# One set of 64x64 score products per tile, keys and queries of the two head halves on row halves of shared tiles

## The chip, the core and the metric

The kernel runs on one core of a Trainium2 chip. The metric is device time in microseconds (us). PE is TensorE, DVE VectorE, ACT ScalarE, POOL GpSimd, SP SyncE, whose queue issues the DMA transfers.

## The reference

Four batches of eight heads, 768 positions, head width 64. Each position attends to a window of 15 positions on either side and to 24 block summaries (the block's largest key, its mean value); a layer norm and a two-layer network with a residual follow.

```python
B, H, S, D = q.shape                      # 4, 8, 768, 64
block, window = (32, 16)
k_sum = k.reshape(B, H, nb, block, D).max(axis=3)
v_sum = v.reshape(B, H, nb, block, D).mean(axis=3)
scores_l = scale * np.matmul(q, k.transpose(0, 1, 3, 2))
mask_l = np.abs(pos[:, None] - pos[None, :]) < window
scores_s = scale * np.einsum('bhsd,bhnd->bhsn', q, k_sum) + np.log(block)
# softmax over both kinds of scores, then a @ concatenate([v, v_sum])
x = np.ascontiguousarray(attn_out.transpose(0, 2, 1, 3)).reshape(B, S, H * D)
xn = (x - mu) / np.sqrt(var + 1e-06) * g_ln
ch = np.maximum(xn @ w_ch1, 0.0) @ w_ch2
return x + ch
```

## The kernel before

**Tiles and stages.** A tile T is 128 positions with all eight heads; there are 24, six a batch. Batch 0 (T = 0 to 5) runs in f32 (steps early_k, early_qk, softmax, early_transp, early_pv), while the weights are fetched, merged and split into f16 high and low parts. Batches 1 to 3 (T = 6 to 23) run with high and low f16 parts. T has two head halves, hh = 0 and 1, of four heads (j) each; t = 2T + hh.

**A late tile.** load_q(t) (line 419) brings the queries of one half into the staging tile qs, twice, once into each 64 of the 128 partitions, with two transfers of 128 KB. ACT casts them to f16 in all 128 partitions, DVE overwrites the first 64 with the low part. load_k(t) (432) brings the keys of the window, already doubled over the two partition halves, in one transfer of 368 KB into ksg; ACT makes kh, DVE the low part kl. heads(T, hh) (455) multiplies over 128 rows, so that a product with kh adds low and high queries at once: for each j, one product with kh and one with kl for either half of the 64 output columns, which begin at key columns that fit that half of the positions. These are 16 products of 128 rows by 64 columns, with 120 moving columns, into one PSUM bank, s0 for hh = 0 and o0 for hh = 1. late_softmax(t) (503) masks and takes the minimum on DVE, exponentiates on ACT, splits into high and low on ACT and POOL, and turns the result by a transposing DMA. values(T) (469), called two tiles later (LAG), has 48 products of 128 rows by 64 columns over 64 moving columns (o). late_out(T) (610) normalises, ln(T) (622) and lnT(T) (638) make the layer norm and turn it by a transposing DMA into xt, of which one covers two tiles, a group g.

**The network.** g1(s) (758), with s = 8g + j, makes 256 hidden columns for a group in two halves of 12 products of 128x128 over 256 columns (h). g2 and, from group 3, g2_wide (827) multiply by the second weights; a g2_wide step has 21 products of 256 columns (acc_a, acc_s, acc_o).

**Batch steps.** batch_k, batch_q, batch_v (294 to 368) load a batch ahead of its tiles and find block summaries and scales; batch_kput (405) casts the key summaries into the border columns of kh and kl of one head half; four POOL copies for each second pair of heads double the summaries over the partition halves (318).

**The order.** The steps don't issue at once. Plan.record notes each operation, a unit() of products counting as one, and issue() (158) emits them in the order of a packed table, ORDER (58): each number in it is the place of an operation in the noted list. The engines' queues run in that order. All instructions carry line 163 for this reason.

**Buffers.** work() (173) gives a tag and a number of buffers to the pool. qs and ksg have one buffer; the f16 queries one for each hh; late["k", hh] is one pair kh, kl for each hh.

Of the kernel before, what the change touches and what calls it, by code (L numbers as in the profile page):

```python
# [13 lines left out]
F32 = mybir.dt.float32  # L14
# [10 lines left out]
P = 128  # L25
# [5 lines left out]
NC = 184  # L31
# [27 lines left out]
    "c-lRf2Y8O>+s3c^36Vr%#9p-`{EZ4RG7v>+O3~J))cg=lt+raNRn=;#)i$<P`Pb~Qil`A1TVj<8DMjqjBqWi%_x1gr*LQqJjyLamp8LMWd7jsKze"  # L59
    "Z}wHEk&8^}G}6aip5$YZ394LiK1-$>Mc!UYF(5yXq^Y<)Zpas9fih05RUbbxvQ8k+QtnrL)XtTT1q-k*1QWRU}F_>k`Mva8FzLM@vZ^xvRaMuRJx"  # L60
    "Sr?c3Tt$%anEHl~GAcj<DtS3pQnlm<CL*)fIrvdUrUzAha_f!kCDW3$%0Uc>l>^*HO_w<gIVbus;mFICz>q<S7VJ~ZSvM6r;vX3=dikgcyR5Ep#^"
    "R}nAJmijtT0*k9I*QeQ*H^?xRR7U>Cevo9kF*w#RO5LLHEGB?H?*3hv3_}(r{iUqPBMk|cTI2(c^a7%-D)SwA@<9at@bB*M_Zd_T3e>;44I~}a#u"
    "R*32iPX)R7XzP{m}~a5=8u>vwWVbM!ZDBc)i~-&E8qdQ-beh8WG4CpJOX$r<h7Z1!|^vTUlgQjc0iI|-g9@<3aA>%NBCoYT?HLmQ=wWVEj2eFS@*"
    "kwJP=Rom)N36uJ!DADiH`X<WzX%nfgE2M<^)23;E<E!_zq*-g<Hbx8R=rY@d-Zn9ZwUt^8aFXe40~2V1ZEgKlqMUzi5jm!@W}AJ<_}d)0V;f4gN%"
    "q7_5qWG%+UxWuM$eG@Sv^PhFR<Q5X~~{HN?*-3mpzxIpB~p6;NvJr>dGr41@<^73lnRDoG5!;&+2jM$Z7^u9FthHMWa=1O$lVJIeJPf%T28yxAX<"
    "sp^k~Aa!X9K475i<XnEPqXZ69}0proiR`sT&Xm16%rh!f4wMrj*-_)@_lE&VLb-w;A`!!Eq))WvIDNXf|9047X`i1$%ZZ#g8&3!{ORgan&^)r$7b"
    "IFpP^3<m22ijN$%QKy%du5FF2R)(sgS@R*B!owv8WU&Z$hC`Bloe77)})w1eaR-tYq|@hwIau4Q`=rLF?KF{Z(`jcwvSnFmzW}&ua9kIr>U(cYh<"
    "?+(FR)4MC)O?*&dF?N*Hy@w6#nnDW{pbLGDONzDd!?GQ;jSskSGTIxbapsp$$gO6UP|&`yEZjvSVK`m$8itLBh>AU)K|UfUV|z9JEtA;shi=>r0c"
    "{4KY=+}aAZXUexkdrRg>I|<gBa#lPVYcFUu6Qn8df3b8HAFV=dOKAhSDV6mD(_K4&gGJJd=Rc@+dC=Qj|3Y8x>OE>zS9h3lME<@$;xAI;%?^8jJ4"
    "5BNey3N=7W=yS$~rJ9TocS|wwkLGFeF53Xrcs~r+n8=ugXy=uP=kxG)b4f_JC<)Z}aMVU1EJ@r3sNJ8)d#j!8)t^?nf=uaa>y;^vA-NMKVEapn%`"  # L70
    "Vdb^WO7&##g<e0S7v(mz@HgDU(W|T(gVH07k4mIECHO=L_k@f<SrE4Cn3ev{vveHNPn07YFr0Q6kBCXlw0R1l{yYgB~E=i0{hHDOZKPY2tCXDw1C"
    "6V@!Nh7LWT7^7E+r#MJH7TY^GTt7NHag!#2-ipy>xFBQxxsFMlF7O^)KxztwdJ5j!lzH90!q_ba&29+ABEgUG|gnTnd&Jm+o*r2l-65%U22NxQE3"
    "LA3w5rHwKdFr_AlW1iGANp)>4`ylcW<_e`=<}_F0-}X4y$H-Ig)|Qdc_3Y-&)Pj?J)BovEIe%?TZ67TdaV#wtv`Y1^AWbvSx(TF27w$+nX@r^Czw"
    "6vfZ{k2zusG}XTAEaZKF$+ZR2Ou}WA4L28cjdl@Veb+qFVEI-H?FQL_8t&Jo+R^dVFWF})eIIW8b&mBnKj@co(z>-TVtUCsJJ!sz&8XKC{lPXiS9"
    "O3aW&(VS9xU_t$WSLpzqawFP?mWHJN~-YMmx(q%4#cYe_3lAnRc>>)rL7MJ=K^l!<+<LOhZhJ+2`?PrZ`NC2Bv^1W26QV{H1R>$@a9wi9dA|jf1x"
    "<QN|ZV?RoLj^>CoK^pXB{g!xw2!tO#k9s&j;oK<#+SwsHyq?waqPibkm^qTCkt+=u-+CENJ+6EG3=IUrsvUpLh65oragnlX=Y?w2b`ahKqG(qF#0"
    "2-CU)Y+n`;>fSMk9sVC5nJ@2F4FpPnu@+7sqkQyyhp|S^ck#ZYqF@YFU)IhPTD)t&g=)%Md05@`Z)}5tY5JH6zypy=sanJBS@3YcDGqfFIt)v`m^"
    "n7-qnTdxPe$E$OX7{P<q*TDJlUv!6eF2yAXAb)ofjgmvHoiX-qbw<RDpwfuM9IhezY#UK9I@$%M0`G)Y_Vov$WHD_J6|wJQ0IlnY?~99mnHDYsJY"
    "+8E}F$L=$o=)`UI9w;5{8Odd(cXWY#!=xV|Id&`mXS4oLGf~6jEm=)$|5A&#F#MwJ2PP9><49S>x5vP17#fhq{P2<OFlDf;)z-S%l+|Xk3ym@ImF"
    "%=BCZC<cnIr}DxDj)=jP92vbosw}p2?BL|3b2;ZHDV|X5V<-E$67^R$f2E1+>yV`o7LK-E@-{lgaQfQ+LR4)ZUnlatYnoKo`H%fm}ZwfANtfOOhV"  # L80
    "IwWQb&(C!<0!|q}3#54D=*>R}Vr}~rj6Zf%Rm+NF^V?SnE02P{zPQ78@Gy`B{1iG=7N`>iF{g_y*N=NFsmZ|xxyw3D0;I6f}ocTOgmSvg+b0c*G`"
    "5cy3x=w4DNS%gG?$BY(sn*()`MZFctzg<OV7Jb^PtaWH?*w_)FwJwAIo*9`6xO8nuS$0vByUKx+_sg>6<q<o#xgb2xwF0W0IgTi(K_Ns7lN6_!$5"
    "yHu5*ayI6HBQp|Xitdz%gvmrD4uE$Vet)I|9|kqW144`+%eT)OkWFFxps#<12|{Mby?<2n(1!3sy1L-E{Oflhy`573XsxJ!2>*MkP(Z&%AJc+H#o"
    "glYJ@c9xAg#re`RfEZV@`*yH66kO!6`f@tf%0v>!EZos8-KOK5OP(sc>cNgV?9vFA<IzLtR=7Q_7xgWfMJDNZ${FMz%4Bsjx~47hUYCh3MEvoGaq"
    "<S0=uGe0lC42o=9zFCKsJfG7e-c+tHuvyIK|w!MHh>~kx-_1I#c}!5tn0noFc|;%(rY)!iLCWyybjeHIie-;B)&>%^dA0<K<_%`H=Uk$T=6~+<-I"
    "oaBnVqMS#kR(uNAml68EagU=Zujls!v=JrUt5fo+UYOw!~CYz7!YJCqCU(RIeO&0&?7~M|vT~H3(AwKv$ePR~b+4`7Oj-f%5w3Un?>nu~+rfN-Rn"
    "oWd@sYEak{S1{y+KxKzvF*$zy{x^6ITNRF3T}QZAH&xTDC<d`!&(>M(R>_S6Z~8X{q2q-O(*9Yng*WJnf%YFxr3fp!-=Qk&&Pp>m&_-2rg;gkG~L"
    "b=t4C3~@hHc?tnsq$Q<oiyOfX-%J_|M7#rl=N#0+U@0`QIDbn|C(&gR3=X!+E1wGUwbTw*Zt8QK;vRZ-7jAnP+Q-huPPBEI=eXG@qljWfyNniw-g"
    "-(|<$<QJ}s@yvxfAFq6w-e;pDPr36nxt>L3(zKV^h#T~yDm|DWn_%E3l&Kam)u6`RIc){VFS>+B2;Sbp#&%$01Ubbq-xg4hxvW<dkK92f%M@nn2t"
    "LbYul68+0NC-9il#a<V~WI}qPuh_dOlr>Y75SOyZL_{yc|RW@=&PzHj@5Uk$>Sz860X1F@8$zOQ2TnRQrqn&7?m1ejArk48`3*f79W~GMHVC{O;m"  # L90
    "$Q}M<%(VGn**<Ys0R^6z<rVO>t(hPkd9pG>%4swfBhiQdmx);q&#`WZY$$a`aRo`UpRN-WHRpPkf9;@y^<L97(bx^a<=*S&*iIP9q<0g;2(q8MqK"
    "~5+#UMFZ(=FKK1cy$x64^Ys5$YVA5yn~i5KnK^zTbv;LSp7?Ob<d-RadfA3BAQ=IKBsr@=<n#s*YY8HSck5Eg%<9|<0sm-_>x$isF(OIjLtQtkN6"
    "`THfIr>^5;0%S8#73@;9FRCj0E9ZV8frdw+hyeoO`0pcR9u(Mi7l5Vls9F-#64F5iQw!q3zo4(^3YB8vZ&{>XPPP{Dnm^j8?XoA;aPb6>t+O8k9v"
# [73 lines left out]
def body(ctx: ExitStack, tc, qt, qa, qe, kt, ks, va, vb, vs, g_ln, w1, w2, blocks, out):  # L167
# [5 lines left out]
    def work(tag, name, shape, dt=F32, bufs=1):  # L173
        return pl.tile(wp, shape, dt, tag, name, bufs)
# [927 lines left out]
```

## Time and profile before

| | before |
|---|---|
| median of 3 runs | 591.59 us |
| lowest, highest | 590.95, 591.9 us |
| span of the profiled execution | 589.9 us |
| PE busy | 577.5 us, 98% |
| DVE busy | 505.0 us, 86% |
| ACT busy | 437.2 us, 74% |
| POOL busy | 134.6 us, 23% |

The profiled execution is told by its span, from the first to the last instruction; the device time of the runs includes what lies around it. Busy times are sums of the instructions' durations without overlaps; those of PE are modelled at their ends and overlap in the pipeline, so its pace is read from starts. The DMA's busy share falls from 8 or 9 tenths in the first fifth of the span to 5 and less in the second half.

### The profile page before, as it was taken

What the parts mean: (1) busy time and instruction counts of PE and PEld (TensorE: products, weight loads), DVE (VectorE), ACT (ScalarE), POOL (GpSimd) and SP (SyncE); (2) the same over time, 40 slices, a digit from 0 to 9 for tenths busy, and PEclk for the clock granted to TensorE, in tenths of its full rate; (3) what the DMA queues carried; (4) which work ended last, traced back from release to release, by engine and by line L of the source; (5) the groups of instructions that cost most, each with busy time, mean ns of one, the idle gap of its engine ahead of it and who ended that gap; (6) DMA issues with size and microseconds to landing.
All of it is one profiled execution on the core that took longest, in us unless ns stands there. A gap on an engine that the chain in (4) does not pass through costs nothing.

```text
span 589.9 us, 16263 instructions
## 1 busy us (share of the span) xinstructions
PE 577.5 (98%) x6152; PEld 467.0 (79%) x6152; DVE 505.0 (86%) x1326; ACT 437.2 (74%) x1079; POOL 134.6 (23%) x225
## 2 busy tenths in 40 slices
PE   7989999999999999999999999999999999999997
PEld 5557768875555688888889888888788888888886
DVE  4899999999999999899798689898798978676653
ACT  3899998888878789879797665898869476652340
POOL 6142120020114132212414111322311311320101
PEclk9999999999999999999999999999999999999999
DMA  8899899645776568567567363565665522431000
GB/s 298 236 271 306 288 273 259 180 126 143 176 193 170 151 175 172 153 176 169 165 169 165 86 115 100 142 172 139 162 144 138 105 79 64 94 82 37 33 5 37
DMA packets 116260, 90.68 MB, mean 154 GB/s; under 512 B 69597, under 2 KB 100445, under 8 KB 116182
## 3 DMA queue, kind: packets, MB, share of 16 engines
q1 hardware_dynamic: 116182, 89.65, 58.5%
q8 instruction: 48, 0.79, 0.6%
q14 instruction: 30, 0.25, 0.1%
HBM read 67.05 MB, written 6.29 MB: 124 GB/s over the span
## 4 chain that ended last, share of the span: by engine, by line
PE 77%; DVE 8%; DMA 7%; ACT 5%; SPq 2%; issue 1%; ACTq 0%; DVEq 0%
PE h L163 33%; PE acc_a L163 11%; PE a L163 11%; PE acc_s L163 8%; PE acc_o L163 7%; DVE m L163 3%; PE s L163 3%; PE o L163 3%; DMA xt<-x 2%; SPq L163 2%; ACT p L163 2%; DMA qs<-in_qt 1%; DMA qs<-in_ks 1%; DMA raw<-in_w 1%; PE warm L163 1%
## 5 line engine op out<-in xcount | busy, mean ns | idle before, releaser
L163 PE MATMUL h<-xt,w_u 128*128 128x256 f16 x2304 | 263.9, 273 | 1.8 <-DMA xt<-x 1.6
L163 PEld LDWEIGHTS <-w_u 128*128 128x128 f16 x2304 | 224.1, 98 | 32.4 <-issue 2.5
L163 PEld LDWEIGHTS <-h_x 128*128 128x128 f16 x1752 | 169.8, 98 | 46.1 <-DVE h_x L163 0.7
L163 DVE TENSOR_TENSOR h_x<-wide,h_x 128x896 f16<-128x896 f32 x72 | 78.4, 1093 | 17.5 <-ACT h_x L163 16.6
L163 ACT CAST h_x<-wide 128x896 f16<-128x896 f32 x72 | 66.6, 933 | 31.4 <-DVE wide L163 29.9
L163 POOL TENSOR_TENSOR p<-p,p 128x480 f16<-128x480 f32 x36 | 44.8, 1247 | 192.0 <-ACT p L163 153.9
L163 DVE TENSOR_TENSOR wide<-wide 128x128 f32<-128x128 f32 (+1 forms) x224 | 75.4, 345 | 15.1 <-ACT wide L163 12.6
L163 ACT ACTIVATE wide<-h 128x512 f32<-128x512 f32 x72 | 42.5, 590 | 38.4 <-PE h L163 26.7
L163 ACT ACTIVATE p<-p,mn,sv 128x120 f32<-128x120 f32 x144 | 68.6, 477 | 1.3
L163 PE MATMUL acc_o<-w,h_x 128*128 128x256 f16 x408 | 56.0, 273 | 0.0
L163 PE MATMUL a<-w,h_x 128*128 128x512 f16 x240 | 52.6, 379 | 0.0
L163 ACT ACTIVATE bst<-bst 128x384 f32<-128x384 f32 (+2 forms) x55 | 32.3, 588 | 17.2 <-DVE vsum L163 9.7
L163 PE MATMUL acc_a<-mix_x,h_x 128*128 128x256 f16 x324 | 44.9, 273 | 0.0
L163 PE MATMUL acc_s<-mix_x,h_x 128*128 128x256 f16 x324 | 43.9, 273 | 0.0
L163 DVE SCALAR_TENSOR_TENSOR m<-raw,m 128x512 uint32<-128x512 uint32 x64 | 42.6, 685 | 0.1
L163 POOL TENSOR_TENSOR x<-x,uv 128x512 f32<-128x512 f32 x18 | 24.1, 1352 | 80.8 <-DVE uv L163 64.9
L163 POOL TENSOR_SCALAR rs<-mv 128x1 f32<-128x1 f32 x24 | 10.3, 428 | 113.8 <-DVE mv L163 109.4
L163 PE MATMUL acc_a<-w,h_x 128*128 128x256 f16 x216 | 35.8, 273 | 0.2
L163 DVE CUSTOM_DVE_ANT_0 p<-s,mask 128x120 f32<-128x120 f32 x144 | 35.0, 273 | 1.1 <-POOL p L163 1.0
L163 DVE SCALAR_TENSOR_TENSOR kl<-ksg,sv,kh 128x640 f16<-128x640 f32 x36 | 32.2, 895 | 2.2 <-ACT kh L163 1.9
L163 DVE SCALAR_TENSOR_TENSOR v<-vst,sv,v 128x512 f16<-128x512 f32 x36 | 27.9, 775 | 3.8 <-ACT v L163 3.8
L163 ACT ACTIVATE kh<-ksg,sv 128x640 f16<-128x640 f32 x36 | 29.4, 818 | 1.3 <-DMA ksg<-in_kt 1.3
(138 smaller groups left out, 886.7 us busy)
## 6 DMA issues: line engine op xcount, KB each, us to landing
raw<-in_w SPq DMA_DIRECT2D x32, 512.0 KB
ksg<-in_kt SPq DMA_DIRECT2D x36, 368.0 KB
qs<-in_qt SPq DMA_DIRECT2D x72, 128.0 KB
out_x<-x SPq DMA_DIRECT2D x24, 256.0 KB
bst<-in_ks SPq DMA_DIRECT2D x20, 192.0 KB
bst<-in_qa SPq DMA_DIRECT2D x15, 256.0 KB
bst<-in_vs SPq DMA_DIRECT2D x20, 192.0 KB
vst<-in_va SPq DMA_DIRECT2D x36, 96.0 KB
```

The lines of the kernel that those rows point to most:

```text
L163: getattr(getattr(nc, engine), op)(*a, **k)
```

## The change

Batches 1 to 3 alone are concerned. load_q and load_k are called once a tile. The queries of hh = 0 stand in partitions 0 to 63, those of hh = 1 in 64 to 127; ACT makes the high part in one tile (qh), DVE the low part over all 128 partitions in another (ql). The keys likewise: two transfers of 184 KB fill the two partition halves of one staging tile, which is cast once; late["k", T % 2] now goes by the tile's parity. heads(T) is one unit for both halves: for each j, high by high, low by high and high by low, for two column halves (r) and two row halves (h): 48 products of 64 rows by 64 columns over 120 moving columns, the row halves into different banks (s0, o0). The product of the two low parts, which was part of the kl product, is no longer formed. Both head halves' softmaxes follow heads(T). The key summaries are stored once for each half, with two POOL copies instead of four; batch_kput(b) fills both parities with the same number of operations. work() makes the tags of several buffers itself, in turn.

The order table has 2955 places instead of 3111. Unpacked, it gives TensorE in batches 1 to 3 18 units of scores and 18 of values, where there were 36 and 18. If the forms 128x128, 128x64 and 64x64 are counted as three, PE changes its form 57 times from the first late scores on (56 before) and 38 times ahead of them (43 before). The first score units stand as before among the steps of groups 2 and 3 of the network. As an instance, around values(17) PE's new list is: values(17), heads(19), half of g1(63), g2_wide(60), g2_wide(61), the other half of g1(63), then g1(64), the first step of the group that needs tile 17. Between values(19) and the first step of group 9 stand half of g1(70), g2_wide(67) to (69) and g1(71); between values(21) and that of group 10 heads(23), g1(79), g2_wide(75) to (77); then come g1(81) and g1(80), group 10; between values(23) and that of group 11 g2_wide(83) to (86) and 12 products of g2_wide(87).

```diff
     @pl.step
-    def load_q(t):
-        T, hh = divmod(t, 2)
+    def load_q(T):
         qs = stg('qs', [P, 4, P])
-        for half in range(2):
-            nc.sync.dma_start(qs[D * half : D * half + D], qt[T, hh])
-        qhl = work(f"qhl{t % 2}", f"qhl{t}", [P, 4, P], F16)
+        nc.sync.dma_start(qs[:], qt[T].rearrange("h d j p -> (h d) j p"))
+        qh, ql = (work(f"qhl{i}", f"q{n}{T}", [P, 4, P], F16) for i, n in enumerate("hl"))
         sc = bt["s", T // NT][:, 1:2]
-        nc.scalar.activation(qhl[:], qs[:], AF.Copy, scale=sc)
-        nc.vector.scalar_tensor_tensor(qhl[:D], qs[:D], sc[:D], qhl[:D], ALU.mult, ALU.subtract)
-        st[t, "q"] = qhl
+        nc.scalar.activation(qh[:], qs[:], AF.Copy, scale=sc)
+        nc.vector.scalar_tensor_tensor(ql[:], qs[:], sc, qh[:], ALU.mult, ALU.subtract)
+        st[T, "q"] = (qh, ql)

     @pl.step
-    def load_k(t):
-        T, hh = divmod(t, 2)
-        ksg = work("qke", f"ksg{t}", [P, 2, 2, NC])
-        nc.sync.dma_start(ksg[:], kt[T, hh].rearrange("r p u c -> p r u c"))
+    def load_k(T):
+        ksg = work("qke", f"kst{T}", [P, 2, 2, NC])
+        for hh, r in enumerate(halves):
+            nc.sync.dma_start(ksg[r], kt[T, hh, :, :D].rearrange("r p u c -> p r u c"))
         x = ksg.rearrange("p r u c -> p (r u) c")[:, :, : P + BLK]
-        kh, kl = (k[:, :, NB : NM - NB] for k in late["k", hh])
+        kh, kl = (k[:, :, NB : NM - NB] for k in late["k", T % 2])
...
     @pl.step
-    def heads(T, hh):
-        t = 2 * T + hh
-        ps = psum(("s0", "o0")[hh], f"s{t}", [P, 512])[:, : 4 * NK].rearrange("p (j c) -> p j c", j=4)
+    def heads(T):
+        pss = [
+            psum(n, f"s{2 * T + hh}", [P, 512])[:, : 4 * NK].rearrange("p (j c) -> p j c", j=4)
+            for hh, n in enumerate(("s0", "o0"))
+        ]
+        q, k = st[T, "q"], late["k", T % 2]
         with pl.unit():
             for j in range(4):
-                for n, k in enumerate(late["k", hh]):
+                for n, (x, y) in enumerate(((0, 0), (1, 0), (0, 1))):
                     for r, c in zip(halves, (0, NB + D)):
-                        nc.tensor.matmul(
-                            ps[r, j], st[t, "q"][:, j, r], k[:, j, c : c + NK], start=(n == 0), stop=(n == 1)
-                        )
-        st[t, "s"] = ps
+                        for ps, h in zip(pss, halves):
+                            nc.tensor.matmul(
+                                ps[r, j], q[x][h, j, r], k[y][h, j, c : c + NK], start=(n == 0), stop=(n == 2)
+                            )
...
     def work(tag, name, shape, dt=F32, bufs=1):
-        return pl.tile(wp, shape, dt, tag, name, bufs)
+        if bufs > 1:
+            rounds[tag] = rounds.get(tag, -1) + 1
+            tag = f"{tag}_{rounds[tag] % bufs}"
+        return pl.tile(wp, shape, dt, tag, name)
...
         if T < TT:
-            for t in two:
-                load_q(t)
-                load_k(t)
+            load_q(T)
+            load_k(T)
...
         if T < TT:
+            heads(T)
             for hh in range(2):
-                heads(T, hh)
                 late_softmax(2 * T + hh)
```

## Rows read from the trace of the kernel before

**Rows 1.** The page, part 1: busy us, share, instructions of PE and PEld.
```profile
PE 577.5 (98%) x6152; PEld 467.0 (79%) x6152; DVE 505.0 (86%) x1326; ACT 437.2 (74%) x1079; POOL 134.6 (23%) x225
```

**Rows 2.** Table by stage: stretch, its length, busy us by engine, PEclk, DMA share, GB/s.
```profile
120.00:586.00 466.00, 464.60 (x5079) 384.31 (x5076) 396.58 (x1000) 334.80 (x757) 103.31 (x113) 1.00 0.51 126
0.00:120.00 120.00, 112.59 (x1076) 82.58 (x1076) 107.66 (x327) 102.36 (x323) 31.32 (x112) 1.00 0.91 262
```

**Rows 3.** Waits of PE: us in total, times, longest us.
```profile
PE h L163 <- DMA xt<-x: 1.6, 2, 1.1
```

**Rows 4.** Timeline of PE, 342 to 350 us: start us, us from first to last.
```profile
342.25 0.82 PE L163 MATMUL acc_o<-w,h_x 128*128 128x256 f16 x6
343.00 0.95 PE L163 MATMUL o<-v,pt 128*64 128x64 f16 x48
343.78 0.22 PE L163 MATMUL s<-kh,qhl 128*64 128x120 f16 x2
...
344.15 0.22 PE L163 MATMUL s<-kl,qhl 128*64 128x120 f16 x2
344.30 5.41 PE L163 MATMUL h<-xt,w_u 128*128 128x256 f16 x48
349.55 0.49 PE L163 MATMUL acc_a<-w,h_x 128*128 128x256 f16 x3
```

**Rows 5.** Groups of PE's instructions by shape: count, busy us, mean ns.
```profile
L163 PE MATMUL s<-kh,qhl 128*64 128x120 f16 x288 | 18.9, 219 | 0.1
L163 PE MATMUL s<-kl,qhl 128*64 128x120 f16 x288 | 18.5, 216 | 0.0
```

**Rows 6.** Timeline of PE, early attention, 82 to 90 us.
```profile
82.39 0.60 PE L163 MATMUL pp<-ident,p 128*128 128x128 f32 x4
82.83 1.36 PE L163 MATMUL h<-xt,w_u 128*128 128x256 f16 x11
...
89.39 0.67 PE L163 MATMUL s<-spare_x,spare_x 64*64 64x128 f32 x16
89.99 0.39 PE L163 MATMUL h<-xt,w_u 128*128 128x256 f16 x2
```

**Rows 7.** Groups of DVE and ACT, 120 to 586 us: count, busy us, mean ns.
```profile
L163 DVE SCALAR_TENSOR_TENSOR kl<-ksg,sv,kh 128x640 f16<-128x640 f32 x35 | 31.3, 896 | 2.2 <-ACT kh L163 1.9
L163 DVE SCALAR_TENSOR_TENSOR qhl<-qs,sv,qhl 64x512 f16<-64x512 f32 x35 | 27.2, 777 | 2.7 <-ACT qhl L163 2.6
L163 ACT ACTIVATE kh<-ksg,sv 128x640 f16<-128x640 f32 x35 | 28.6, 818 | 1.3 <-DMA ksg<-in_kt 1.3
L163 ACT ACTIVATE qhl<-qs,sv 128x512 f16<-128x512 f32 x35 | 25.0, 713 | 2.8 <-DMA qs<-in_qt 2.5
```

**Rows 8.** Chain that ended last, 395 to 421 us: start us, us, what.
```profile
395.08 3.80 DMA qs<-in_qt
...
402.20 4.72 DMA qs<-in_qt
...
415.01 4.84 DMA xt<-x
419.89 1.16 PE h L163 x9
```

**Rows 9.** Timelines of PE, DVE and SP, 225 to 238 us, around tile 9.
```profile
225.79 0.95 PE L163 MATMUL o<-v,pt 128*64 128x64 f16 x48
...
237.35 0.82 PE L163 MATMUL h<-xt,w_u 128*128 128x256 f16 x6
...
226.78 0.69 DVE L163 TENSOR_TENSOR x<-o,lrc 128x512 f32<-128x512 f32 x1
...
229.24 0.75 DVE L163 SCALAR_TENSOR_TENSOR xn<-x,mv,gb 128x512 f32<-128x512 f32 x1
...
232.15 0.74 DVE L163 SCALAR_TENSOR_TENSOR x<-xn,rs,x 128x512 f16<-128x512 f32 x1
...
232.92 1.88 SPq L163 DMA_TRANSPOSE xt<-x  x1
```

More of the change, by code (lines that the diff above doesn't have):

```diff
@@ L64 @@
[L64 to L93, printed above, removed]
@@ L314, in batch_k @@
         if hp == 0:
-            bt["k", b] = work("ksum", f"ksum{b}", [P, 4, 2, NB], F32, 2)
-        t = bt["k", b]
+            bt["k", b] = work("ksum", f"ksum{b}", [P, 2, 2, NB], F32, 2)
         if hp % 2:
+            hh = hp // 2
             for j in range(2):
-                for half in range(2):
-                    nc.gpsimd.tensor_copy(
-                        t[half * D : half * D + D, hp - 1 : hp + 1, j, :], m[j * D : j * D + D, hp - 1 : hp + 1]
-                    )
+                nc.gpsimd.tensor_copy(
+                    bt["k", b][hh * D : hh * D + D, :, j, :], m[j * D : j * D + D, hp - 1 : hp + 1]
+                )
     @pl.step
@@ L404, in batch_kput @@
     @pl.step
-    def batch_kput(b, hh):
-        src = bt["k", b][:, 2 * hh : 2 * hh + 2].rearrange("p a j n -> p (a j) n")
-        kh, kl = late["k", hh]
+    def batch_kput(b):
+        src = bt["k", b].rearrange("p a j n -> p (a j) n")
         sc = bt["s", b][:, 2:3]
-        for c in (0, NB + P + BLK):
-            nc.scalar.activation(kh[:, :, c : c + NB], src, AF.Copy, scale=sc)
-            nc.vector.scalar_tensor_tensor(
-                kl[:, :, c : c + NB], src, sc, kh[:, :, c : c + NB], ALU.mult, ALU.subtract
-            )
+        for kh, kl in (late["k", i] for i in range(2)):
+            for c in (0, NB + P + BLK):
+                nc.scalar.activation(kh[:, :, c : c + NB], src, AF.Copy, scale=sc)
+                nc.vector.scalar_tensor_tensor(
+                    kl[:, :, c : c + NB], src, sc, kh[:, :, c : c + NB], ALU.mult, ALU.subtract
+                )
@@ L454, in heads @@
     @pl.step
-    def heads(T, hh):
-        t = 2 * T + hh
-        ps = psum(("s0", "o0")[hh], f"s{t}", [P, 512])[:, : 4 * NK].rearrange("p (j c) -> p j c", j=4)
+    def heads(T):
[4 more added lines that the diff above has]
+        q, k = st[T, "q"], late["k", T % 2]
         with pl.unit():
             for j in range(4):
-                for n, k in enumerate(late["k", hh]):
+                for n, (x, y) in enumerate(((0, 0), (1, 0), (0, 1))):
                     for r, c in zip(halves, (0, NB + D)):
-                        nc.tensor.matmul(
-                            ps[r, j], st[t, "q"][:, j, r], k[:, j, c : c + NK], start=(n == 0), stop=(n == 1)
-                        )
-        st[t, "s"] = ps
+                        for ps, h in zip(pss, halves):
+                            nc.tensor.matmul(
+                                ps[r, j], q[x][h, j, r], k[y][h, j, c : c + NK], start=(n == 0), stop=(n == 2)
+                            )
+        for hh in range(2):
+            st[2 * T + hh, "s"] = pss[hh]
     @pl.step
@@ L1036, in body @@
             batch_mask(b)
-            for hh in range(2):
-                batch_kput(b, hh)
+            batch_kput(b)
         if T < NT:
```

72 lines of the change are left out of this document (49 added, 23 removed).

## Prediction

> **What bounds the kernel now.** I read the profile from the whole to the part. TensorE (PE) is busy 98% of the span, far ahead of the others [rows 1]. The table by stage says where it is not: in the first 120 us it is busy 112.59, so some 7.4 us are open there; from 120 to 586 us it is busy 464.60 of 466.00, at the full granted clock, while VectorE (DVE) has 397 and ScalarE (ACT) 335 [rows 2]. A busy PE need not be a PE at its pace, so I checked the pace on starts: 48 products of a hidden-layer step (h) begin at 344.30 and the next group at 349.55, 5.25 us or 0.109 us each [rows 4], 256 columns at 2.4 GHz with little on top. What PE still waits for is short: the longest waits outside the first microseconds are two for the transposed layer-norm rows (xt), 1.6 us together [rows 3]. So from about 120 us on a microsecond that leaves PE's own list leaves the time, and a microsecond that leaves DVE, ACT or the DMA queue is worth nothing, unless it shortens one of those waits. The output work after the last products is not touched by the change.
>
> **The products.** A tile's scores are today 32 products of 128 rows by 64 columns over 120 moving columns (16 with kh, 16 with kl). Two that go to the two column halves run side by side: their starts come as pairs, and from the first pair at 343.78 to the eighth at 344.15 there are 0.37/7 = 0.053 us a pair [rows 4], which is 120 columns at 2.4 GHz, 0.050, and 0.003 more. 18 tiles have 576 products in all [rows 5], so 288 pairs, 15.2 us of PE. The change has 48 products a tile, of 64 rows by 64 columns, in 12 sets of four, one for each quarter of the array: 216 sets. If a set takes what a pair takes, these are 11.4 us, and **3.8 us** go. The early attention shows sets of that form, in f32: 16 products begin at 89.39, the next h at 89.99, so four cost at most 0.60/4 = 0.15, or 0.126 with one change of form (0.095, below) taken off, while one 128-column f32 product alone takes (82.83 - 82.39)/4 = 0.11 [rows 6]. Four at once there cost hardly more than one. Bounds for the f16 set: 0.053 below, 0.105 above (row halves in turns), and between them 0.065, four products at the pace of the 64-column ones (o), which need (343.78 - 343.00)/48 = 0.016 each [rows 4]. I take 0.053, since the f32 sets, of the same shape, lie at the lower end.
>
> By the Trainium skill, "TensorE: Matmul & The Clock Gate", Part 3, packed products cost the duration of one and about 4 ns for each further tile: 0.062 for a set, 13.4 us in all, and the time would be 589.3; its chance is in that of rival (b). The pairs here, at 0.053, show no such addition beside the 0.050 of the columns. The same part's table has sixteen 32x32 tiles at 10.6 times the rate of one, so it speaks for row halves that run at once in f16; no row here shows that.
>
> **The changes of form.** Going from the 128x128 form into a column-split one costs PE: six acc_o products begin at 342.25 and the first o at 343.00, 0.75 - 6 x 0.109 = 0.095 us more than their pace; going back, the last s at 344.15 and h at 344.30 are 0.15 apart instead of 0.053, 0.097 [rows 4]. Between o and s, both 128 rows by 64, there is no step: 48 o products fill 343.00 to 343.78 without a gap [rows 4]. The unpacked orders have 56 changes of form behind the first late scores before and 57 after, if one between 128x64 and 64x64 counts too; ahead of it 43 and 38. Net 4 fewer, **0.4 us** less. If that new kind of change were free, 15 more would go, 1.4 us; if it cost twice, 1.4 us would come. The Trainium skill, "TensorEngine Tiling (Array Packing)", Key Properties, has every change of tiling mode drain TensorE, which by itself would make it one change, as counted.
>
> **Conversions, loads, copies.** Half of 36 query and 36 key conversions go: on ACT 18 x (0.713 + 0.818) = 27.6 us, on DVE 18 x (0.777 + 0.896) = 30.1 us [rows 7]. The remaining DVE one for queries works on 128 partitions instead of 64, but on the same 512 columns; the key row, 128 partitions and 640 columns in 0.896, allows no more than that for it. SyncE (SP) issues three transfers a tile instead of six, with 624 KB a tile less. None of this is on PE's list. What it can return are waits that it caused: the chain from 395 to 420 us runs through two query loads that wait for the one staging tile (3.80 and 4.72 us to land), then the layer-norm chain of tile 17 and its transposing DMA, at whose end h starts at 419.89 [rows 8]. PE lost 1.1 us there, the longer of its two xt waits [rows 3], and 1.4 in all after 120 us [rows 2]. I take **1.4 us** as what the lighter load returns; bounds 0 and 3, as pieces too short to be counted as idle may be as much again. The GpSimd copies (12 fewer) and the tags made by hand in work(), which rotate as the pool's did, I cost at nothing: PE's surplus hides them, and were that cover gone they would save, not add.
>
> **The added wait.** heads(T) now waits for both banks (s0, o0) and all conversions of the tile before its first product; behind it PE's whole list stands. Between two heads the order has ten or more microseconds of other products, against 0.713 + 0.777 us that query conversion needs after the earlier scores released its tiles [rows 7]. I cost it at nothing; a late load would show as up to 4.72 us, the longer of the two landings above.
>
> **The new order** places hidden steps nearer to the rows that they need. From values(T) the path is: normalising (late_out), layer norm on DVE, GpSimd, DVE, ACT, DVE, then a transposing DMA, then g1. For tile 9 it took from the end of its o products (225.79 + 0.95) to h at 237.35, 10.6 us, without a stop of PE [rows 9]. Of these, 226.78 to 229.99 went from the normalising to the centred row, 3.2 us; an ACT cast (0.713, as in [rows 7]) and the low part (0.74) follow, 4.7 us in all if no foreign work stands between, as it did there until 232.15; the DMA from its issue at 232.92 had at most 4.4 [rows 9]. Tile 17's took 4.84 and PE waited [rows 8]. So an undisturbed path is about 9.1 to 9.6 us, an estimate from these rows. In the new order the work between values(17) and g1(64) is heads, 0.053 x 12 + 0.19, two g1 halves of 12 products and two g2_wide of 21, 66 x 0.109: 8.0 us. PE would wait 1.1 to 1.6 there; I take **1.3**. For groups 9, 10 and 11 the same count gives 10.8, 10.3 and 10.5, enough if the path stays near 10. The early stage I leave as it is: 7.4 us are open there [rows 2], its order is new in many places, and either sign is as good; I allow 2 us each way for the range.
>
> **Sum.** -3.8 - 0.4 - 1.4 + 1.3 = -4.3 us on the profiled execution's 589.9 us, so a span of 585.6. The median of the runs, 591.59, is 1.7 above the span, for what lies around it: **587.3 us**.
>
> **Rivals.** (a) Row halves take turns in f16. For it: an output partition of the f32 sets gets 2 x 128 results in 0.11 to 0.126 us, and one of the f16 pairs 120 in 0.053, both about 2.3 a ns; f16 sets at 0.053 would need 4.5 a ns, which nothing in the trace shows [rows 4, 6]. Against it: different banks, and the f32 rows. A set would take 0.105, 216 of them 22.7 us: +7.5 - 0.4 - 0.1 = +7.0, **598.6**, slower. It decides from 15.7/216 = 0.073 us a set. Chance 0.08. (b) Sets at 0.065, by the pace of the o products: 14.0 us, -1.2 - 0.4 - 0.1 = -1.7, **589.9**. Chance 0.12. (c) The layer-norm path is the late one: with a length L the waits before groups 8 to 11 are L less 8.0, 10.8, 10.3 and 10.5. At 10.6 they are 3.0 us (2.6 at group 8), still faster; from L = 11.3, 5.6 us, nothing is left, and at 12.5 they are 10.4 us: -3.8 - 0.4 - 1.4 + 10.4 = +4.8, **596.4**, slower. For it: tile 17's chain ran through 13 us of other engines' work and DMA before its h [rows 8]. Against it: DVE has 30 us less to do and PE's order leaves it alone behind these tiles. Chance 0.10. (d) More comes back than I count: the early stage's open time shrinks by 2 us with an order made for fewer conversions and transfers, **585**. Chance 0.10.
>
> **How the numbers follow.** The forecast has 0.60: 585 to 589.5. Runs of this kernel lie within 0.95 us, so a change within 0.2% (1.2 us) can't be told from none. Faster by over 0.2% (under 590.4): 0.57 of the forecast, (d) 0.10, (b) 0.08: 0.75. Within: 0.10, from (b), the forecast's upper tail and a mild (c). Slower: (a) 0.08 and most of (c): 0.15. The range reaches from (d) with the free changes of form, 583.5, over (b) to the near part of (c), 591.
>
> **What would show it.** Right: s products in fours with sets 0.053 apart, 12 to a tile; about 0.095 at every change of form, at that between values and heads too; DVE and ACT some 30 and 27 us less busy with no trace of it in the span; a short PE wait before g1(64), near 410 to 415 us. Wrong: sets at 0.07 or more, or PE waits of over 5 us behind 120 us, on xt or on the query tiles.

## The result, and the profile after

| | before | after |
|---|---|---|
| median of the runs, us | 591.75 (590.95 to 592.03) | 599.12 (598.17 to 601.15) |
| span of the profiled execution, us | 589.9 | 596.4 |
| last product ends, us | 586.35 | 592.66 |

The ratio after to before is **1.0130, 95% interval 1.0107 to 1.0154**: slower, by 7.7 us of 592. The forecast was 587.3, and its range ended at 591.

The page of the changed kernel, part 1 (against [rows 1]), and its table by stage (stretch, its length, busy us by engine, granted clock, DMA share, GB/s; against [rows 2]):

```profile
PE 576.2 (97%) x6440; PEld 466.1 (78%) x6440; DVE 488.9 (82%) x1290; ACT 413.9 (69%) x1043; POOL 128.8 (22%) x213
```

```profile
0.00:120.00 120.00, 110.04 (x1033) 80.19 (x1034) 103.10 (x312) 97.94 (x311) 30.19 (x108) 1.00 0.86 257
120.00:592.00 472.00, 465.54 (x5406) 385.56 (x5404) 384.77 (x977) 315.96 (x733) 98.57 (x105) 1.00 0.43 101
```

Every engine is less busy than before, the DMA queues move less, the clock is granted in full, and the kernel is longer. The reader is to look at PE's column in the second row: behind 120 us 6.46 us are open, where before there were 1.40; in front of it 9.96, before 7.41. That is 7.6 us of new idle time; what is in front of 120 us turns out below to differ as much between traces of one and the same early order. The new idle time is in no one place. PE's waits (us in total, times, longest):

```profile
PE gain L159 <- DMA xn<-in_g_ln: 4.2, 1, 4.2
PE low L159 <- DVE diag L159: 1.3, 1, 1.3
PE h L159 <- DMA xt<-x: 1.1, 1, 1.1
PE o L159 <- DMA vst<-in_va: 1.0, 1, 1.0
PE s L159 <- DMA spare_x<-in_qe: 0.9, 1, 0.9
PE h L159 <- ACT wide L159: 0.9, 2, 0.7
PE o L159 <- DVE v L159: 0.8, 2, 0.6
PE h L159 <- DVE x L159: 0.8, 1, 0.8
PE s L159 <- DVE ql L159: 0.8, 2, 0.6
```

Before, two xt waits of 1.6 us together were the largest entry behind the wait of the first microseconds (gain, 3.6 us) [rows 3]. Now many instructions, ended by DVE, ACT and the DMA queue alike, each come 0.3 to 1.3 us late. What PE has to do did get shorter: if each product is given the time that its kind takes at its steady pace, and the rest between two starts is counted as lost, the products need 556.9 us before and 553.4 after (3.5 less), and 25.9 us are lost before, 35.1 after (9.2 more). These four are estimates from the starts: they depend by up to 1 us on how a kind's pace is taken. So two questions: were the 3.5 us those that were forecast, and where do the 9.2 come from.

The products first. The timeline of PE around one late tile (start us, us from first to last):

```profile
360.64 0.82 PE L159 MATMUL acc_o<-w,h_x 128*128 128x256 f16 x6
361.39 0.25 PE L159 MATMUL s<-kh,qh 64*64 64x120 f16 x4
361.46 0.22 PE L159 MATMUL s<-kh,ql 64*64 64x120 f16 x4
361.52 0.22 PE L159 MATMUL s<-kl,qh 64*64 64x120 f16 x4
...
361.99 0.22 PE L159 MATMUL s<-kl,qh 64*64 64x120 f16 x4
362.14 0.63 PE L159 MATMUL o<-v,pt 128*64 128x64 f16 x28
```

From the second set at 361.46 to the twelfth at 361.99 there are 0.53/10 = 0.053 us a set, what a pair took before [rows 4]; within a set the four starts lie 3 or 4 ns apart. The first set of a unit is longer, 0.077. From the last acc_o to s and from the last s to o it is 0.095 to 0.1 us more than the pace.

### The profile page after: what moved, and what is told of

Same layout as the page of the kernel before. It is cut to its first block, busy times and chain, and to the rows that moved or that the text cites. A ratio compares the mean times of both kernels' runs of the same rounds, so it can differ in the third digit from the quotient of the medians.

```text
span 596.4 us, 16606 instructions
## 1 busy us (share of the span) xinstructions
PE 576.2 (97%) x6440; PEld 466.1 (78%) x6440; DVE 488.9 (82%) x1290; ACT 413.9 (69%) x1043; POOL 128.8 (22%) x213
## 4 chain that ended last, share of the span: by engine, by line
PE 41%; DVE 12%; ACT 6%; DMA 4%; issue 3%; SPq 1%; POOL 0%; ACTq 0%; DVEq 0%; POOLq 0%
PE h L159 20%; PE acc_a L159 8%; PE acc_s L159 6%; PE acc_o L159 5%; DVE h_x L159 3%; DVE wide L159 3%; DMA bst<-in_ks 2%; ACT p L159 2%; ACT h_x L159 2%; PE o L159 1%; DVE x L159 1%; SPq L159 1%; PE s L159 1%; DVE p L159 1%; ACT wide L159 1%
## 5 line engine op out<-in xcount | busy, mean ns | idle before, releaser
L159 DVE TENSOR_TENSOR h_x<-wide,h_x 128x896 f16<-128x896 f32 x72 | 80.6, 1128 | 23.5 <-ACT h_x L159 23.0
L159 DVE TENSOR_TENSOR wide<-wide 128x128 f32<-128x128 f32 (+1 forms) x224 | 78.8, 363 | 19.8 <-ACT wide L159 17.5
L159 DVE CUSTOM_DVE_ANT_0 p<-s,mask 128x120 f32<-128x120 f32 x144 | 36.9, 274 | 7.6 <-POOL p L159 7.6
L159 POOL TENSOR_SCALAR rs<-mv 128x1 f32<-128x1 f32 x24 | 12.8, 534 | 112.0 <-DVE mv L159 103.8
L159 ACT ACTIVATE v<-vst,sv 128x512 f16<-128x512 f32 x36 | 25.4, 712 | 4.9 <-DMA vst<-in_va 3.3
L159 DVE SCALAR_TENSOR_TENSOR v<-vst,sv,v 128x512 f16<-128x512 f32 x36 | 27.5, 767 | 1.2 <-ACT v L159 1.2
L159 ACT ACTIVATION_READ_ACCUMULATOR p<-p,mn,sv 128x1 f32 x144 | 27.0, 188 | 0.0
```

Of the source, the lines that this page charges most:

```text
L159: getattr(getattr(nc, engine), op)(*a, **k)
```

## The experiments

Unless it is said otherwise an edit is made to the kernel with the changed steps. The cost of the order is the difference of two kernels whose steps are equal. Runs of one kernel spread more widely than the 0.95 us that I had from three: the 25 runs of the kernel before that were taken beside the first of these experiments lie between 590.35 and 594.5 us.

### The steps without the order

The changed steps, with the places of the old order: a step that replaces two takes the place of the first of them, and is moved only where its data isn't there yet.

```diff
-ORDER = (the new order)
+ORDER = (the old order, its places carried over to the 2955 new ones)
```

> The changed steps with the order of before carried over: every operation that both kernels have keeps its place, the one load and the one group of scores of a tile stand where the first of the two stood, and an operation moves only where data forces it. Theory O, the new order makes TensorE wait: the waits go and the lighter list shows, 3.8 us for the sets of four, 0.0 to 1.4 us for the lighter load, some of it lost where the old order had two groups apart: 586 to 589 us. Theory S, the changed steps themselves make TensorE wait (one group needs both banks and every conversion of its tile): the time stays near that of the changed kernel, 596 us or more. Theory T, the hand-made tags cost: near 596 us as well.

Measured: **589.39** (588.08 to 592.41), ratio to before 0.9956 [0.9936, 0.9977]. That is 0.4 us over the range of theory O. The steps alone are faster than before, by 2.6 us; the order alone turns that into a loss. Between this kernel and the changed one, with the same instructions, lie 1.74% or 10.3 us (9.7 between the medians), give or take 1.8 us by the two intervals. By its median it is also the fastest of the kernels here that leave nothing out. Its table by stage and its PE waits behind 120 us:

```profile
0.00:120.00 120.00, 109.53 (x1025) 79.21 (x1026) 104.62 (x315) 98.21 (x313) 27.61 (x108) 0.99 0.88 258
120.00:586.00 466.00, 465.10 (x5411) 385.31 (x5410) 376.62 (x974) 315.78 (x731) 96.95 (x105) 1.00 0.43 102
```

```profile
PE s L157 <- DVE mn L157: 0.4, 1, 0.4
PE h L157 <- ACT wide L157: 0.3, 1, 0.3
```

Behind 120 us 0.90 us are open, against 6.46. PE, ACT and the DMA queue do what they do in the changed kernel; DVE is busy for 8 us less with the same instructions, which comes back below.

The first row has to be read with care. The profiled execution took 592.41 us, 3 us over the median. In its first 120 us 10.47 us are open, more than in the changed kernel; behind a wait of 2.3 us for xt the granted clock fell to the lower of its two levels, 1.2 GHz, from 114.4 to 117.8 us, and the h products there lie 0.213 us apart instead of 0.109. Such stretches come in other traces too, each time in or right behind a wait of PE. In the traces of the kernels below that share this early order, 6.7 to 10.5 us are open in the first 120; where the early order is the new one, 6.7 to 10.1. So the traces show what the order does behind 120 us, and what it does in front of that can be read from the medians alone.

### One half new, one half old

The order is cut at the first late scores (near 124 us): old in front and new behind, and the reverse.

```diff
-ORDER = (new)
+ORDER = (old up to heads(6), new behind it)       # e2; e3: new up to it, old behind
```

> The changed steps; up to the first late scores in the order of before, from there on in the new one. Theory O: TensorE was idle 9.96 us in the first 120 us against 7.41 before, so 2 to 3 us come back, and the later waits stay: 595 to 598 us. Theory S or T: no more than 1 us from the changed kernel, 598 to 600 us.

> The changed steps; up to the first late scores in the new order, from there on in that of before. Theory O: the later waits go (idle 6.46 us in the 472 us behind 120 us, against 1.40 in 466 us before), the early 2.5 us stay: 588 to 592 us, and with e2 and e1 the parts add up. Theory S or T: 596 us or more.

Measured: e2 **606.69** (ratio 1.0237 [1.0173, 1.0301]), e3 **592.89** (1.0008 [0.9983, 1.0032]). From e1 to e3, only the early part made new, 0.52% or 3.1 us; from e3 to the changed kernel, the late part made new, 1.22% or 7.2 us, each give or take 2 us; e3 is 0.9 us over its range. The late part is seen in the traces as well: without added work the old late order leaves 0.4 to 3.5 us open behind 120 us (e1, e3 and the variants of e1 below), the new one 4.6 to 8.7. The other way round it doesn't add up: with the old early part the new late one costs 17 us. PE's longest waits in e2:

```profile
PE h L157 <- DVE h_x L157: 4.2, 1, 4.2
PE h L157 <- DMA xt<-x: 3.4, 2, 3.2
```

The 4.2 us stand at 125 us, right behind the cut: the new late part expects steps to be done that the old early part has not yet reached. My 595 to 598 for e2 missed that. Part of the 17 us is the clock: it was at 1.2 GHz from 128.3 to 135.1 us and from 428.7 to 432.1, in and behind these two waits, which costs at most half of 10.2 us, an estimate.

### The tags alone

The kernel before with only the hand-made rotation of tags in work().

```diff
+        if bufs > 1:
+            rounds[tag] = rounds.get(tag, -1) + 1
+            tag = f"{tag}_{rounds[tag] % bufs}"
```

> The kernel before with one edit: tags of several buffers are made by hand in turn, as the change does. Theories O and S: nothing, 591 to 592.5 us. Theory T: several us slower, 595 us or more.

Measured: **591.62**, ratio 0.9997 [0.9980, 1.0013]. Nothing, as forecast.

### Row halves in turn

The steps in the old order (e1), the twelve sets of four taken apart: all products of one row half, then all of the other.

```diff
-            for j in range(4):
-                for n, (x, y) in ...:
-                    for r, c in zip(halves, (0, NB + D)):
-                        for ps, h in zip(pss, halves):
+            for ps, h in zip(pss, halves):
+                for j in range(4):
+                    for n, (x, y) in ...:
+                        for r, c in zip(halves, (0, NB + D)):
```

> The changed steps in the old order (e1), but a tile's 48 products first all of the upper row half, then all of the lower: 24 pairs instead of 12 sets of four. If a set of four takes what a pair takes (0.053 us) and TensorE's list is the path, 12 x 0.053 = 0.63 us a tile come on top, 11.4 in all: 600 to 602 us. If the row halves had been taking turns anyway, or were hidden, nothing: 589 to 590 us.

Measured: **597.33** (1.0078 [1.0060, 1.0096]), 7.9 us over e1. In its trace the 48 starts of a tile span 1.058 us where e1's span 0.612; 18 x 0.446 = 8.0 us. By the ratios it is 7.2 us, and either is uncertain by some 1.6; within that the price is found in the products, and that PE's list is the path in this order holds. One tile of the trace:

```profile
382.07 0.24 PE L157 MATMUL s<-kh,qh 64*64 64x120 f16 x2
382.15 0.22 PE L157 MATMUL s<-kh,ql 64*64 64x120 f16 x2
...
382.52 0.22 PE L157 MATMUL s<-kl,qh 64*64 64x120 f16 x2
382.53 0.26 PE L157 MATMUL s<-kh,qh 64*64 64x120 f16 x4
382.60 0.23 PE L157 MATMUL s<-kh,ql 64*64 64x120 f16 x4
382.66 0.23 PE L157 MATMUL s<-kl,qh 64*64 64x120 f16 x4
382.71 0.22 PE L157 MATMUL s<-kh,qh 64*64 64x120 f16 x2
...
383.13 0.22 PE L157 MATMUL s<-kl,qh 64*64 64x120 f16 x2
```

From 382.15 to 382.52 there are 0.37/7 = 0.053 us a pair, and 0.053 again from 382.71 to 383.13: a pair of one row half takes what a set of four takes. What my 600 to 602 missed is the seam. In the rows of four the last three pairs of the first half run beside the first three of the second: the second half's first pair begins 0.453 us after the tile's first product, and three pairs of the first half, which stand ahead of it in the kernel, begin behind it, the last at 0.601. In the one tile whose second half had to wait for its semaphore, the first half's 24 products begin within 0.605 us and the second half's behind them. Three pairs of the second half thus cost nothing. Rival (a) of the forecast is settled against.

### The load

e1 with every late conversion done twice, at its place; then with DVE's half of it twice, and ACT's half.

```diff
-        nc.scalar.activation(qh[:], qs[:], AF.Copy, scale=sc)
+        with pl.unit():
+            for _ in range(2):                       # e6, e13; e12: 1
+                nc.scalar.activation(qh[:], qs[:], AF.Copy, scale=sc)
-        nc.vector.scalar_tensor_tensor(ql[:], qs[:], sc, qh[:], ALU.mult, ALU.subtract)
+        with pl.unit():
+            for _ in range(2):                       # e6, e12; e13: 1
+                nc.vector.scalar_tensor_tensor(...)  # and both for the keys
```

> The changed steps in the old order (e1), with each cast of late queries and keys done twice in a row, so that ScalarE and VectorE have their 27 and 30 us again; transfers and products are those of e1. If the lighter load is worth the 1.4 us of the prediction: 589.5 to 592.5 us. If it is worth nothing: e1's 589.4 within 1 us. If the old order's fit rested on it: 594 us or more.

> The changed steps in the old order, each late conversion's DVE half (the low parts of keys and queries) done twice, ACT's half once: some 30 us more of DVE work, none of ACT. With both done twice the kernel took 627.0, 37.6 more than once. Theory D, DVE is the engine that has no room: 610 to 622, most of the 37.6. Theory A, ACT is: under 594. Theory E, both queues pass it on alike: 600 to 610.

> The same with ACT's half (the high parts) done twice and DVE's once: some 27 us more of ACT work. Theory D: 590 to 595. Theory A: 610 to 622. Theory E: 600 to 610.

Measured: e6 **627.03** (1.0588 [1.0568, 1.0608]), e12 **612.15** (1.0333 [1.0309, 1.0358]), e13 **598.71** (1.0111 [1.0092, 1.0131]). Against e1 that is 37.6, 22.8 and 9.3 us. e12 lies where the theory that DVE has no room had it; e13 is over that theory's range and under the one for both queues, so ACT passes on a part as well. The added work, from the groups of the changed kernel (count, busy us, mean ns, 120 to 592 us; against [rows 7]),

```profile
L159 DVE SCALAR_TENSOR_TENSOR kl<-kst,sv,kh 128x640 f16<-128x640 f32 x17 | 16.1, 946 | 0.5 <-ACT kh L159 0.5
L159 DVE SCALAR_TENSOR_TENSOR ql<-qs,sv,qh 128x512 f16<-128x512 f32 x18 | 14.8, 822 | 1.5 <-ACT qh L159 1.5
L159 ACT ACTIVATE kh<-kst,sv 128x640 f16<-128x640 f32 x17 | 13.9, 818 | 2.1 <-issue 2.1
L159 ACT ACTIVATE qh<-qs,sv 128x512 f16<-128x512 f32 x17 | 12.1, 710 | 0.0
```

is 18 x (0.946 + 0.822) = 31.8 us on DVE and 18 x (0.818 + 0.710) = 27.5 on ACT. So of a microsecond added to DVE at these places 0.7 come out at the end, of one added to ACT 0.3, of both at once 0.6. A part of this is the clock, which was at 1.2 GHz behind long waits of PE for 3.4 us in e12's trace and 13.7 in e6's: at most half of that, 1.7 and 6.8 us, an estimate. Yet neither engine is full. The stretch from 120 us of e12, and its four largest PE waits behind the first microseconds:

```profile
120.00:606.00 486.00, 466.83 (x5382) 382.94 (x5382) 408.59 (x1004) 312.41 (x723) 102.64 (x105) 1.00 0.41 98
```

```profile
PE s L157 <- DVE mn L157: 4.5, 4, 2.3
...
PE s L157 <- DVE kl L157: 3.0, 2, 1.5
PE acc_a L157 <- DVE h_x L157: 2.9, 4, 1.1
PE a L157 <- DVE x L157: 2.8, 1, 2.8
```

DVE still idles for 77 of 486 us, and PE waits for it all the same. I read it so: DVE works its list from the front, an instruction whose data isn't there yet holds up all behind it, and so the idle time lies at other places than the added work. That is argued from the waits and not tested by itself. The waits fall on scores, hidden-layer parts and accumulators alike.

### The batch steps moved across

The steps that summarise batches 2 and 3 (batch_k, batch_q, batch_v) are put at the amount of PE work at which the other order has them: old times in the new order (e8), new times in the old one (e9). The mean shift is 5 us.

```diff
-ORDER = (new)              # e9: (old)
+ORDER = (new, batch_k, batch_q, batch_v of b > 1 by the old order's time)
```

> The changed kernel in its new order, but the loads and block sums of batches 2 and 3 (batch_k, batch_q, batch_v, with one staging tile in a ring of transfer, VectorE and ScalarE) stand where TensorE's progress has them in the old order; they move by 5 us on the mean. If these steps, standing in the queues ahead of urgent work, make the late waits: half of the 6.2 us between the changed kernel and e3 or more come back, 593 to 596 us. If the waits come from many places: 597 to 600 us.

> The counterpart: the changed steps in the old order (e1), with the same loads and block sums of batches 2 and 3 where TensorE's progress has them in the new order. If they make the late waits: 592 to 596 us. If not: 589 to 591 us.

Measured: e8 **617.03** (1.0413 [1.0375, 1.0451]), 18 us over the changed kernel, e9 **598.16** (1.0101 [1.0063, 1.0138]), 8.8 over e1. Both miss upwards. Neither place is the better one: either is bad within the other order, and moving these steps made two further orders, whose late waits are many (behind 120 us 25 us are open in e8). I take it that an order is a fit of all steps to one another.

### SyncE's queue

The 44 loads of the one staging tile (bst) for batches 2 and 3 go to ACT's queue, in the new order (e10) and in the old one (e11).

```diff
-        nc.sync.dma_start(x[:], qa[b, :, c * DM : c * DM + DM])
+        (nc.scalar if b > 1 else nc.sync).dma_start(x[:], qa[b, :, c * DM : c * DM + DM])
```

> The changed kernel with its own new order; the loads of the staging tile of batches 2 and 3 (key blocks, queries, values for the batch means) are issued by ACT instead of SP, each at its place in the order, so that SP no longer stands still behind them until ACT has squared the tile before (81.6 us of such waits in the changed kernel's SP queue, 61.6 before). Theory R, the new order loses its time in SP's queue, where the layer norm's transfers stand behind these loads: 590 to 595. Theory Q, it loses it in the places of the steps in the queues of DVE and ACT, and SP only passes that on: 597 to 602, no better than the changed kernel's 599.1.

> The changed steps in the old order, with the same loads of batches 2 and 3 on ACT's queue: the control for the run above. Theory R: within 2 us of 589.4 for the kernel without it, since that order loses nothing there (late PE idle 0.9 us). Theory Q: the same, or up to 3 us more if ACT's issues stand in the way of its own work.

Measured: e10 **598.68** (1.0109 [1.0084, 1.0134]), e11 **591.36** (0.9979 [0.9951, 1.0007]). SP's 81.6 us of waits for ACT's squares fall to 7.7, and the time stays where it was. That these loads stand in SP's queue is not the cause. SP's queue as a whole isn't cleared by this run, since other waits in it grew: for DVE's x from 73.0 to 98.6 us, for POOL's p from 28.7 to 50.3.

### VectorE held by GpSimd

The 8 us more of DVE in the new order led here. DVE and POOL, 345 to 350 us of the changed kernel:

```profile
346.66 1.08 DVE L159 TENSOR_TENSOR h_x<-wide,h_x 128x896 f16<-128x896 f32 x1
347.66 1.50 DVE L159 TENSOR_TENSOR wide<-wide 128x256 f32<-128x256 f32 x1
```

```profile
346.83 2.05 POOL L159 TENSOR_TENSOR x<-x,uv 128x512 f32<-128x512 f32 x1 [1.99 <-DVE uv L159]
```

POOL's addition begins while DVE's h_x runs and takes 2.05 us, where the mean is 1.36; DVE's next instruction meets the addition and takes 1.50 us where it takes 0.42 alone; it ends at 349.16, 0.28 behind POOL's end. Most held instructions end so: 0.15 us behind POOL for 128 columns, 0.28 for 256, 0.55 for 512, 0.95 for 896. Held are mostly DVE instructions with two operands in SBUF that begin while one of POOL's subtractions (p) or additions (x) runs, and a few short ones with a scalar from SBUF (lrc, 0.64 us longer at 403 us); the scores' p<-s,mask that met a subtraction, with one operand from PSUM, took at most 7 ns more than their median. By the Trainium skill, "SBUF — State Buffer", Who interferes with whom, a DVE instruction with two SBUF inputs contends with a GpSimd one that reads SBUF, and not with one that only writes it. The traces agree, the latter in e16 and e17. If each DVE instruction is compared with the median of its form, and what is over by more than 40 ns is summed behind 120 us, DVE was held for 7.3 us before, 16.7 in the changed kernel and 11.3 in e1; so 5.4 of the 8 us are holds. Two pairs of runs test what that is worth: POOL's instructions in pieces, and a fill in their place (the low part of the probabilities and a part of the residual sum are then left out).

```diff
-        nc.gpsimd.tensor_tensor(lo, p, hi, ALU.subtract)
+        for j in range(4):                                  # e14, e15; the additions likewise
+            nc.gpsimd.tensor_tensor(lo[:, j : j + 1], p[:, j : j + 1], hi[:, j : j + 1], ALU.subtract)
+        nc.gpsimd.memset(lo, 0.0)                           # e16, e17 instead
```

> The changed kernel with POOL's subtraction of the probabilities' high part (128x480, 1.22 us) and its addition to the output rows (128x512, 1.35 us) each cut into four pieces (the second addition into two). In the changed kernel VectorE instructions with two inputs in SBUF that meet one of these last up to 1.1 us longer, 16.7 us in all behind 120 us. Theory H, these holds carry the new order's loss and a hold ends with the piece: holds under 8 us, 590 to 595. Theory P, the loss is in the places of the steps, holds or not: holds under 8 us but 597 to 600. If VectorE isn't let in between two pieces, the holds stay at 15 us or more and the run says nothing of the theories.

> The changed steps in the old order with the same pieces. Holds 11.3 us behind 120 us without them. Theory H: 586 to 588.5, holds under 6 us. Theory P: 588.5 to 591.

> The changed kernel with a fill of zeros on POOL in place of that subtraction and of those additions: the low part of the probabilities and the residual with two of the products are left out of the result. A fill reads no SBUF. Theory H: VectorE's holds behind 120 us fall under 4 us, and the time to 586 to 591, within 2 us of the same edit in the old order. Theory P: holds fall alike, the time stays over 594, 6 to 10 us over the same edit in the old order.

> The changed steps in the old order with the same fills, the same parts left out: both theories 585 to 588.5, and it is the yardstick for the run above.

Measured, new order and old: pieces **602.02** (1.0166 [1.0134, 1.0198]) and **590.58** (0.9980 [0.9959, 1.0000]), holds 9.3 and 6.4 us; fills **595.33** (1.0057 [1.0036, 1.0078]) and **587.58** (0.9929 [0.9909, 0.9948]), holds 0.9 and 2.2. The pieces shortened the holds and gained nothing, and e14 is over both its ranges; but POOL itself was busy for 35 us more behind 120 us (133.9 us in e14), and the wait for xt before g1(64) grew from 1.1 to 3.3 us, with the clock at 1.2 GHz from 419.7 to 423.1 in and behind it, so this pair settles little. With the holds all but gone the new order gains 0.73%, the old one 0.27%: of the 10.3 us between them 2.7 go and 7.6 stay. The 2.7 are uncertain by some 2.5 us, by the four intervals. The stretches behind 120 us, fills in the new and in the old order:

```profile
120.00:590.00 470.00, 465.37 (x5406) 385.59 (x5405) 369.72 (x978) 315.53 (x733) 56.69 (x105) 1.00 0.42 101
```

```profile
120.00:582.00 462.00, 461.23 (x5360) 381.93 (x5348) 365.38 (x963) 311.68 (x723) 53.87 (x105) 1.00 0.44 103
```

PE idles for 4.6 and 0.8 us. The theory that the holds carry the loss falls; they are about a quarter of it, and at most a half.

### The staging tile's loads

The chain that ended last between 238 and 247 us, and PE there:

```profile
238.96 3.73 DMA bst<-in_ks
242.70 0.02 issue
242.72 0.56 DVE kmax L159
```

```profile
244.59 0.92 PE L159 MATMUL o<-v,pt 128*64 128x64 f16 x46 [0.27 <-DVE v L159]
245.44 0.25 PE L159 MATMUL s<-kh,qh 64*64 64x120 f16 x4
246.31 0.25 PE L159 MATMUL s<-kh,ql 64*64 64x120 f16 x4 [0.62 <-DVE ql L159]
```

DVE's maximum stands still for a load that could go out only when ACT had squared the tile before; the conversions of values and queries behind it in DVE's list come late, and PE waits in the midst of a tile's scores. Behind 130 us DVE and ACT wait 9.0 us for such loads in the new order, 2.8 in the old one. Such waits need not cost PE anything: in the kernel before they are 7.7 us, and PE has 1.4 us open. So the 44 loads are left out; the tile is filled once with ones, and the summaries of batches 2 and 3 are then those of ones.

```diff
-                kk = stg(...)
-                nc.sync.dma_start(kk, ks[b, hp, :, cs])
+                kk = kept[...]          # b > 1: one tile of ones; queries and values likewise
```

> The changed kernel in its new order without the 44 loads of the staging tile for batches 2 and 3: the tile is filled once with ones, and the maxima, sums and squares of these batches are taken of it at their old places, so that their results are not those of the inputs. Theory L, the new order loses its time where VectorE and ACT wait for these loads (9 us of such waits behind 130 us in the changed kernel, 2.8 in the old order): 590 to 594.5, within 4 us of the same edit in the old order. Theory P, the places of many steps each cost a little, and the loads are only one of the waits that show it: 595 to 598.5, 6 to 10 us over the same edit in the old order.

> The changed steps in the old order with the same loads left out, the same results changed: both theories 587 to 589.5, and it is the yardstick for the run above.

Measured: **596.10** (1.0077 [1.0053, 1.0101]) and **588.12** (0.9942 [0.9924, 0.9960]). The gap goes from 10.3 to 8.0 us; that is 2.3, uncertain by some 2.5, so the loads carry a quarter or nothing. A second staging tile wasn't tried.

## Why the prediction was wrong, step by step

**The bound** was read rightly, but for one sentence. PE's list sets the end, as e5 shows within its noise (7.9 us by the medians, 8.0 by the products), as long as what PE needs comes in time.

**Sets of four at 0.053, -3.8; changes of form, -0.4: right.** Sets are 0.053 apart, the changes of form cost 0.095 to 0.1, that between 128x64 and 64x64 among them, and PE's products need 3.5 us less in all. The Trainium skill, "TensorE: Matmul & The Clock Gate", Part 3, adds some 4 ns for each further tile; the starts within a set show them, the distance of the sets, 0.053, does not. Rivals (a) and (b) are out. (The low end of the range, 583.5, is 583.6 by its own terms, 585 less 1.4; nothing rests on it.)

**The lighter load, -1.4: wrong, and so was the sentence under it.** The terms without the new order add up to 5.6 us less. In the old order, where PE loses 0.9 us behind 120 us, the steps gave 2.6 us (1.4 to 3.8), and the products alone account for 3.5, or 4.2 with the changes of form as forecast: of the 1.4 at most 0.3 came back. And "worth nothing" was no property of the load. I had read from PE's 464.60 of 466.00 [rows 2] that DVE and ACT had room. What it shows is only that this order hid these durations: e12 adds a load of the size of the one that was removed, and 0.7 of it comes out. DVE's busy time fell by 16.1 us and not by 30.1, ACT's by 23.3 and not 27.6; 9.4 of DVE's missing 14 are holds by POOL.

**The added wait, 0.** Right in its kind: the unit of scores was stopped in the middle at 246.31 and once more near 478, 1.2 us together, and waited 0.3 for its tiles at 308. In the old order one unit was stopped likewise, for 0.6 us at 290 (e1). Small, but not nothing.

**The new order, +1.3: this is the step that failed.** The wait that it was made of is there, and of the size forecast. The chain and PE's timeline around g1(64), which answer to [rows 8]:

```profile
410.40 0.88 PE o L159 x48
...
415.03 0.61 ACT x L159
...
416.98 3.36 DMA xt<-x
420.34 0.14 issue
420.47 1.58 PE h L159 x13
```

```profile
417.87 1.47 PE L159 MATMUL h<-xt,w_u 128*128 128x256 f16 x12
420.47 1.25 PE L159 MATMUL h<-xt,w_u 128*128 128x256 f16 x10 [1.13 <-DMA xt<-x]
```

1.1 us were lost there, 1.1 to 1.6 were forecast, and groups 9 to 11 cost nothing, as counted; the kernel before lost the same 1.1 us there [rows 3, 8]. From the end of the o products, 411.28, to h at 420.47 there are 9.2 us, where 9.1 to 9.6 were estimated. (In other traces with this order the same wait is 2.2, 2.9 and 3.3 us, in e18, e10 and e14, and nothing in e16.) But the order as a whole cost 10.3 us, not 1.3. I had costed an order of 2955 places by the one path that I could follow on PE's list, left the lists of DVE, ACT, POOL and SP unread, and set the early part, "either sign as good", to 0 within 2 us. Measured, the late part costs 7.2 us and the early one 3.1, each give or take 2. The sign of failure that the forecast named, PE waits of over 5 us behind 120 us, has come in their sum (6.46 us open), but on ACT's wide and DVE's v, x and ql as much as on xt. Rival (c) had the sign and the mechanism of one path; the loss isn't on one path.

**What of the 10.3 us is explained.** Holds of DVE by POOL 2.7 and loads of the staging tile 2.3, each uncertain by some 2.5; the forecast layer-norm wait 1.1 (read from the trace alone); the staging loads' place in SP's queue nothing. The 1.1 is no further term: in e16, without the holds, no wait stands before g1(64). If the holds and the loads don't overlap, which wasn't run, 5.0 us are explained. The rest, 5 us or more, stays open. Behind 120 us it is seen as waits of 0.3 to 0.8 us on many instructions. The early part's 3.1 us are in no trace: the longest early wait behind the start in the changed kernel is 1.3 us, for diag, which scales the weights, and e1's trace has longer ones. That an order has no single culprit fits e2 and e8, mixtures of the two orders that are worse than either, and e9, 8.8 us over the order that it was made from; e3, a mixture too, lies between the two. It isn't shown for each wait.

## What to carry over

A full column of the busiest engine says that the order hides all else at its present durations, and not that the others have room. I would now price a change of load or of order by how far each hidden step's result lies ahead of its use, on the list of every engine; that wasn't tried here. Where a change brings new steps and a new order, run the new steps in the old order first; here that is the faster kernel, and the order alone cost 10 us. Look at the granted clock of each stretch and at the spread of the runs before a single trace is taken for the kernel: two traces here with one early order differ by 3.8 us of open time in the first 120. When DVE and POOL share a stretch, look whether instructions with two SBUF operands on both sides meet, since their durations then belong to the order too; here that was worth 2.7 of 10.3 us at the most likely.

## What was not expected of the hardware

A DVE instruction of 0.42 us took 1.50 beside a GpSimd addition, and the addition 2.05 where it takes 1.36: in this pair each waits for the end of the other. A change of order alone made DVE's held time 16.7 us instead of 11.3 (e1). Four 64x64 products on the four quarters are as quick as a pair on one row half, 0.053 us, and products of one row half begin ahead of products of the other that stand before them in the kernel: in e5 the second half's first pair begins at 0.453 us, the first half's last at 0.601. Behind some waits of PE the granted clock fell to 1.2 GHz for a stretch (2.3 us in e1, 114.4 to 117.8); behind the 2.9 us in e10 it did not.
